# Pooled attention, two gated layers, one core: the second pass gets its own tiles for squares and rows, more raw tiles, and a later load of the plain block's weights

## The chip, the core and the metric

The kernel runs on one NeuronCore of a Trainium2 chip. The metric is the device time of one execution in microseconds. A second execution is recorded by the hardware profiler; all rows shown here are from that one.

## What is computed

Three layers follow each other on 4608 tokens (8 batches of 576), all in float32:

```python
k_p, v_p = mean of k, v over 8 neighbours;  attn = softmax(q @ k_p.T / 8) @ v_p
x   = attn, heads side by side                      # 4608 x 512
h   = (x @ w1) * (x @ w2)                           # 4608 x 1024
y   = (h @ w3) @ w_out                              # 4608 x 512
xn  = y / sqrt(mean(y*y, -1) + 1e-6) * rms_g
out = (silu(xn @ w_gate) * (xn @ w_val)) @ w_out2   # inner width 1536
```

Every matmul is done on pairs of float32r tiles, a rounded part ("hi") and the rest ("lo"), in three products (helper mm3, lines 104 to 106).

## The kernel before

The inputs are taken in 9 blocks of 512 tokens, and the program has four stages.

**First pass.** While w3 @ w_out is multiplied out to one matrix wp, attention for batch 0 runs; then for each block the function ab makes h, feature by feature, between pieces of the attention for the next batch. Eight blocks store h in memory (hdram); the ninth keeps it on the chip (h8).

**Second pass.** Nine turns, in the order of blocks 8, 4, 5, 6, 7, 0, 1, 2, 3 (the list OB); the text calls them turn 0 to turn 8. A turn has eight steps m, each of four groups of three matmuls of y = wp.T @ h: 96 matmuls. For every second step one piece of h (128 x 1024) is loaded by SyncE's queue (h_load, tile hr, 3 buffers), cast by ACT and subtracted by DVE into a pair hb (h_split, line 1315, 4 buffers). The four results of a turn stand in four PSUM banks; turns alternate between two pools of four banks. At the end of a turn y_end squares the four banks (ACT, L670), copies them out (L678 and L680), stores them, and adds up the squares (DVE, L684). During the next turn the list todo is worked off, one entry per step: sq_split makes a hi and lo pair of the sum of squares (L690, L692), four entries do nothing, then rms multiplies by a vector of ones (L698, L699; the result is put in a bank of the pool that the finished turn used), copies the one row to the chip's memory (L701, "the row copy"), and stores it (sdram<-f, L702, "the row store"). GpSimd's queue loads it back (L704), DVE scales it (L705), GpSimd takes the power -0.5, and stores it to rdram (L709). Block 0, of turn 5, needs its row again during turn 7, as xn_load (L1017) and xn_split (L1027 to L1031).

**Weights prepared beside it.** The gate, value and output weights are turned from float64 words to float32, combined and split by the steps of Conv, gv_steps and o2_steps. From the ninth block on these are called by the Ticker named side, one call per step, 82 calls for 97 entries; the results go to memory in stores of 1 MB on GpSimd's queue (wd, od). Raw words are loaded by SyncE's queue into the tiles xq (2 buffers), and for the output weights also into four tiles cut from the pool x0 (oraw). All float32 work tiles named f, 128 x 512, come from one pool of 5: the squares, the hi and lo of their sum, the row, the raw words' work tile, and later the results of the plain block.

**Third stage.** Block 0 goes plainly through the gated layer (gv, o_mm); its weights are pieces wr, 8 loads of 512 KB that pre_ring issues in turn 0 from step 4. Its results are copied out by put(0), called through end0 inside the first product of the last stage. The other eight blocks go in pairs through a scheme of seven products (quad, o_part) whose sums stand in the tiles acc.

A scheduler orders the instructions on each engine; an engine works its own list strictly in order. The excerpts below are from those lists.

Of the kernel before, what the change touches and what calls it, by code (L numbers as in the profile page):

```python
# [9 lines left out]
F32 = mybir.dt.float32  # L10
# [11 lines left out]
def kernel(  # L22
# [637 lines left out]
    def ybank(i):  # L660
        if turn.get(i, 0) % 2:
            return psum()
        return py_p.tile([P, 512], F32, tag="y", name="y")

    def y_end(i):
        ys = yacc.pop(i)
        sq = []
        for kk in range(KD):
            sq.append(ftile())
            nc.scalar.activation(sq[kk], ys[kk], AF.Square)  # L670
            if i == 0:
                if kk == 0:
                    xr[i, 0] = rtile("xr", F32).rearrange("p (k t) -> p k t", k=KD)
                yc = xr[i, 0][:, kk, :]
            else:
                yc = hxtile("hh" if kk % 2 else "hl").bitcast(F32)
            if kk % 2:
                nc.scalar.copy(yc, ys[kk])  # L678
            else:
                nc.vector.tensor_copy(yc, ys[kk])  # L680
            if i:
                nc.sync.dma_start(out=ydram[i, kk], in_=yc)
            if kk:
                nc.vector.tensor_tensor(out=sq[0], in0=sq[0], in1=sq[kk], op=ALU.add)  # L684
# [11 lines left out]
        def rms():  # L696
            ps = ybank(i) if turn[i] < NB - 1 else psum()
            nc.tensor.matmul(ps[:1], ones, sp[0], start=True, stop=False)  # L698
            nc.tensor.matmul(ps[:1], ones, sp[1], start=False, stop=True)  # L699
            row = ftile()  # L700
            nc.scalar.copy(row[:1], ps[:1])  # L701
# [8 lines left out]

        return [sq_split] + [lambda: None] * 4 + [rms]

# [20 lines left out]
    def xq_raw():  # L733
        return r_ps[0].tile([P, 1024], I32, tag="xq", name="xq", bufs=2)

    def gv_steps(G, s, kp):
# [45 lines left out]

        cs, raws = [], (xq_raw if late else raw_halves())
        for z in range(2):
# [17 lines left out]
    for n, (cs, steps) in enumerate(groups):  # L802
# [3 lines left out]
        if n + 1 not in (4, len(groups)):  # L806
            nxt = groups[n + 1][0]
            steps[4] = lambda f=steps[4], nxt=nxt: (nxt[0].s0(), nxt[1].s0(), f())
        gv_prep += steps
# [64 lines left out]
    def o2_steps():  # L874
        jobs, cells = [], [{} for _ in odram]

        x0raw = []

        def o2_raw():
            if not x0raw:  # L880
                for nm in ("xh", "xl"):
                    t = x0_p.tile([P, KD, TB], F32R, tag=nm, name="oraw").bitcast(I32)
                    t = t.rearrange("p k t -> p (k t)")
                    x0raw.extend([t[:, :1024], t[:, 1024:], None])
            r = x0raw.pop(0)
            x0raw.append(r)
            return xq_raw() if r is None else r

        def row(g, j):
# [4 lines left out]
        for g in range(len(odram)):  # L894
            for j in range(4):
                jobs.append(
                    Conv(
                        w_o2[(4 * g + j) * P : (4 * g + j + 1) * P, :],
                        o2_raw,
                        out=lambda g=g, j=j: row(g, j),  # L900
# [143 lines left out]
    def put(i):  # L1044
        ys = yacc.pop(i)
        for t in range(4):
            o = ftile()
            if t % 2:
# [191 lines left out]
    def o_part(k0, g, i0, steps):  # L1240
        if not accs:
            accs.extend(
                x1_p.tile([P, KD, TB], F32R, tag=nm, name="acc").bitcast(F32)
                for nm in ("xh", "xl")
            )
        X = [psum() for _ in range(2)]
# [66 lines left out]
    for i in range(NB - 2, NB):  # L1313
        for n, (m, s) in enumerate((m, s) for m in range(KF1) for s in range(2)):
# [6 lines left out]
            if i == NB - 2 and n == 10:  # L1321
                for g in range(2):
                    for l, lst in enumerate((wph, wpl)):
                        nc.sync.dma_start(out=lst[g].bitcast(F32), in_=wpdram[g][l])
            if (i, n) > (NB - 2, 13):
                side()
# [7 lines left out]
    for w, i in enumerate(OB):  # L1334
        for m in range(KF1):
# [8 lines left out]
            if m and todo:  # L1344
                todo.pop(0)()
            if w == 0 and m == 4:
                wr += [wtile(wB_p, "wr").rearrange("p k t -> p (k t)") for _ in range(4)]
# [65 lines left out]
    o_mm(0, 2 * NCH - 2)  # L1413
    xn.pop(0)

    def end0():
# [75 lines left out]
```

## Time and profile before

| | us |
|---|---|
| three timed executions: median | 1642.26 |
| lowest, highest | 1640.07, 1647.4 |
| profiled execution, own time | 1649.54 |
| its span, first to last instruction | 1647.5 |
| PE busy in the span | 1595.0 (97%) |
| DVE, ACT, GpSimd busy | 1100.4, 727.3, 85.3 |

PE is busy nearly throughout, so the profile is read for the stretches in which it isn't. A row of a window has the two ends, the length, busy time and instructions of PE, PEld, DVE, ACT and POOL, then the granted share of the TensorE clock (1.00 is 2.4 GHz, a stretch at 1.2 GHz counts 0.5), the busy share of the 16 DMA engines and GB/s. A row of a timeline has start, length, engine, line, operation, tiles, and in brackets the idle time of the engine ahead of it and what ended it.

### The profile page before, as it was taken

How to read it: one execution, taken by the hardware profiler on the slowest of the kernel's cores; microseconds unless marked ns; L12 is line 12 of the kernel's file. 1: busy time of each engine (PE TensorE's matmuls, PEld its weight loads, DVE VectorE, ACT ScalarE, POOL GpSimd, SP SyncE). 2: the span in 40 equal slices, each digit the busy share in tenths (PEclk: the TensorE clock that was granted, in tenths of full speed). 3: DMA queues.
4: the chain of work that ended last, by engine and by line, in shares of the span. 5: the costliest groups of instructions: out<-in, count | busy, mean ns of one | idle time of the engine just before them, and what ended most of it. 6: DMA issues, size and time to landing. Idle time of an engine off the chain costs nothing.

```text
span 1647.5 us, 22285 instructions
## 1 busy us (share of the span) xinstructions
PE 1595.0 (97%) x8114; PEld 1308.0 (79%) x8114; DVE 1100.4 (67%) x1938; ACT 727.3 (44%) x1700; POOL 85.3 (5%) x107
## 2 busy tenths in 40 slices
PE   5899999999999999999899999999999999999998
PEld 2447778877777788887688788988898898898897
DVE  4676698779787158668825264696468747676556
ACT  4776545444442136465523244244335343434422
POOL 1001101010000000111100000000000000000000
PEclk9899999999999999999999999999999999999999
DMA  9858545554571179788777666668666866676652
GB/s 245 259 170 216 114 110 155 132 151 112 147 237 70 65 264 343 257 292 284 272 253 245 192 192 188 202 193 286 187 192 199 287 190 195 197 238 188 194 181 94
DMA packets 191775, 328.96 MB, mean 200 GB/s; under 512 B 52265, under 2 KB 91177, under 8 KB 186034
## 3 DMA queue, kind: packets, MB, share of 16 engines
q1 hardware_dynamic: 172530, 276.10, 53.7%
q0 software_dynamic: 19136, 51.45, 10.7%
q8 instruction: 64, 1.05, 0.3%
q14 instruction: 45, 0.37, 0.1%
HBM read 250.89 MB, written 76.58 MB: 199 GB/s over the span
## 4 chain that ended last, share of the span: by engine, by line
PE 65%; DMA 4%; DVE 3%; issue 1%; ACT 1%; POOL 0%; DVEq 0%; POOLq 0%; ACTq 0%; SPq 0%
PE ps L104 16%; PE ps L105 16%; PE ps L106 16%; PE y L105 3%; PE y L106 3%; PE y L104 3%; PE o L105 2%; PE o L106 2%; PE o L104 2%; DMA sdram<-f 2%; DMA ss<-sdram 1%; PE pa L325 1%; PE pa L428 1%; DVE ost L101 1%; DMA out_dram<-f 0%
## 5 line engine op out<-in xcount | busy, mean ns | idle before, releaser
L104 PE MATMUL ps<-xf,wr 128*128 128x512 f32 x576 | 225.9, 395 | 2.9 <-ACT f L1191 2.8
L105 PE MATMUL ps<-xf,wr 128*128 128x512 f32 x576 | 225.2, 391 | 0.0
L106 PE MATMUL ps<-xf,wr 128*128 128x512 f32 x576 | 224.8, 390 | 0.0
L1071 DVE TENSOR_TENSOR f<-y,f 128x512 f32<-128x512 f32 x48 | 33.1, 690 | 168.0 <-PE y L106 157.2
L368 DVE STREAM_TRANSPOSE aT<-s 32x256 f32<-32x256 f32 x324 | 140.8, 435 | 5.2
L1191 ACT COPY f<-ps 128x512 f32<-128x512 f32 x144 | 84.4, 586 | 127.6 <-PE ps L106 126.5
L104 PEld LDWEIGHTS ps<-xf,wr 128*128 128x128 f32 x576 | 108.5, 188 | 30.4 <-DVE f L1071 5.3
L106 PEld LDWEIGHTS ps<-xf,wr 128*128 128x128 f32 x576 | 108.4, 188 | 23.0
L105 PEld LDWEIGHTS ps<-xf,wr 128*128 128x128 f32 x576 | 108.6, 189 | 21.3
L104 PE MATMUL ps<-xh,w1h 128*128 128x512 f32 x288 | 118.8, 413 | 0.0
L340 ACT ACTIVATE s<-pa,mx 128x72 f32<-128x72 f32 (+1 forms) x280 | 85.4, 331 | 73.2 <-DVE mx L337 73.2
L105 PE MATMUL ps<-xl,w1h 128*128 128x512 f32 x288 | 114.4, 397 | 0.0
L104 PE MATMUL ps<-xh,w2h 128*128 128x512 f32 x288 | 112.8, 392 | 1.4 <-ACT w2h L100 1.4
L106 PE MATMUL ps<-xh,w1l 128*128 128x512 f32 x288 | 113.0, 392 | 0.0
L106 PE MATMUL ps<-xh,w2l 128*128 128x512 f32 x288 | 112.4, 390 | 0.0
L105 PE MATMUL ps<-xl,w2h 128*128 128x512 f32 x288 | 112.2, 390 | 0.0
L634 PE MATMUL wps<-wo,hl 128*128 128x512 f32 x128 | 67.9, 658 | 15.8 <-ACT hl L560 8.4
L572 ACT COPY f<-ps 128x512 f32<-128x512 f32 x72 | 42.9, 599 | 81.0 <-PE ps L106 77.2
L1071 DVE TENSOR_TENSOR f<-ps,f 128x512 f32<-128x512 f32 x96 | 65.0, 687 | 19.8 <-PE ps L106 8.9
L1071 DVE TENSOR_TENSOR acc<-ps,acc 128x512 f32<-128x512 f32 x72 | 48.5, 686 | 33.8 <-PE ps L106 19.1
L106 PE MATMUL ps<-o,hf 128*128 128x256 f32 x240 | 67.9, 283 | 0.0
L105 PE MATMUL ps<-o,hf 128*128 128x256 f32 x240 | 67.9, 283 | 0.0
(244 smaller groups left out, 3934.1 us busy)
## 6 DMA issues: line engine op xcount, KB each, us to landing
wr<-wd SPq DMA_DIRECT2D x168, 512.0 KB
o<-od SPq DMA_DIRECT2D x96, 512.0 KB
wd<-wst POOLq DMA_DIRECT2D x24, 1024.0 KB, 7.1
hr<-hd SPq DMA_DIRECT2D x32, 512.0 KB
od<-ost POOLq DMA_DIRECT2D x12, 1024.0 KB, 7.3
wr<-wd SPq DMA_DIRECT2D x48, 256.0 KB
x1raw<-in_moe_w_dram SPq DMA_DIRECT2D x20, 512.0 KB
hd<-hh SPq DMA_DIRECT2D x36, 256.0 KB
```

What stands on the lines that cost most here:

```text
L101: nc.vector.tensor_tensor(out=lo, in0=src, in1=hi.bitcast(F32), op=ALU.subtract)
L104: nc.tensor.matmul(o, lh, rh, start=first, stop=False, skip_group_check=part)
L105: nc.tensor.matmul(o, lh, rl, start=False, stop=False, skip_group_check=part)
L106: nc.tensor.matmul(o, ll, rh, start=False, stop=last, skip_group_check=part)
L325: nc.tensor.matmul(ps[:n, (p % 2) * 2 * SP : (p % 2 + 1) * 2 * SP], qT_t[t // 2][:, t % 2, p, :n], kT[:, p, :], start=True, stop=True,)
L340: nc.scalar.activation(s_t[t][:n, h, :SP], pv[:, j, :], AF.Exp, bias=mx[:, j, :], accum_out=den_t[t][:n, h, :],)
L368: nc.vector.transpose(aT[32 * kb : 32 * kb + 32, :, s0 + 32 * i : s0 + 32 * i + 32], s_t[t][32 * i : 32 * i + 32, :, 32 * kb : 32 * kb + 32],)
L428: nc.tensor.matmul(ps[j * D : (j + 1) * D, :n], st8["vp", b][:, h * D : (h + 1) * D], st8["aT", b][:SP, h, c0 : c0 + n], start=True, stop= ...
L572: nc.scalar.copy(a0[i, m], ps)
L634: nc.tensor.matmul(wps[i], wt[:, i * P : (i + 1) * P], wo[j // 4][:, j % 4, :], start=j == 0, stop=j == KF1 - 1,)
L1071: nc.vector.tensor_tensor(out=out, in0=in0, in1=in1, op=op)
L1191: nc.scalar.copy(t, bank)
```

## The change

Four things change.

- x0b: the two tiles of pool x0, free after the first pass, are cut into eight pieces. The squares take pieces 0 to 3, the row takes piece 4 or 5 by turn, instead of f tiles. The hi and lo of the sum stay f tiles. rms stands one entry earlier in todo (after step 5 instead of step 6).
- late_raw: at the ninth block, once the first four weight tiles of the first pass (pool wB) are free, they become eight more raw tiles. Late gate, value and output weights take them and the two xq in rotation; the oraw tiles go. The loads of the next group but one are issued when the sums of a group are made.
- The tiles wr, of the same pool wB, are now taken and loaded in turn 8, from step 1 (as the program is written), after the last entry of side.
- put(0) copies into the sum tile acc, which is now taken before the last stage, instead of f tiles.

```diff
+    def bpiece(k):
+        if not x0b:
+            for nm in ("xh", "xl"):
+                t = x0_p.tile([P, KD, TB], F32R, tag=nm, name="x0b")
+                x0b.extend(t[:, u] for u in range(KD))
+        return x0b[k]
-            sq.append(ftile())
+            sq.append(bpiece(kk).bitcast(F32))
-            row = ftile()
+            row = bpiece(4 + turn[i] % 2).bitcast(F32)
-        return [sq_split] + [lambda: None] * 4 + [rms]
+        return [sq_split] + [lambda: None] * 3 + [rms]
+    def late_raw():
+        if not more:
+            return xq_raw()
+        r = more.pop(0)
+        more.append(r)
+        return xq_raw() if r is None else r
-            steps[4] = lambda f=steps[4], nxt=nxt: (nxt[0].s0(), nxt[1].s0(), f())
+            def sums_and_loads(f=steps[4], n=n, nxt=nxt):
+                for n2 in (n + 1, n + 2):
+                    if n2 == n + 1 or (more and n2 < len(groups)):
+                        for c in groups[n2][0]:
+                            if not hasattr(c, "raw"):
+                                c.s0()
+                f()
-            o = ftile()
+            o = accs[0][:, t, :]
+            if (i, n) == (NB - 1, 9):
+                wbt = [wtile(wB_p, "raws").bitcast(I32) for _ in range(4)]
+                for u in range(2):
+                    more.append(None)
+                    for t in wbt:
+                        more.append(t.rearrange("p k t -> p (k t)")[:, u * 1024 : (u + 1) * 1024])
-            if w == 0 and m == 4:
+            if w == NB - 1 and m == 1:
+                side.flush()
                 wr += [wtile(wB_p, "wr").rearrange("p k t -> p (k t)") for _ in range(4)]
```

On ACT, at the end of turn 7. L1030 is a part of block 0's xn_split, hb the cast of a piece of h, ost<-ot the casts of prepared output weights, L701 the row copy, L670 the squares at the turn's end. Before:

```order
L1030 ACTIVATE xnh_6726<-xr,g_col 128x512
L100 CAST hb<-hr 128x1024
L1030 ACTIVATE xnh_6726<-xr,g_col 128x512
L701 COPY f<-y 1x512
L100 CAST ost<-ot 128x2x256
L1030 ACTIVATE xnh_6726<-xr,g_col 128x512
L100 CAST ost<-ot 128x2x256 x3
L670 ACTIVATE f<-ps 128x512 x2
```

Now (L1045, L710 and L679 are the same three lines of code):

```order
L1045 ACTIVATE xnh_6675<-xr,g_col 128x512 x2
L100 CAST hb<-hr 128x1024
L100 CAST ost<-ot 128x2x256 x2
L1045 ACTIVATE xnh_6675<-xr,g_col 128x512
L100 CAST ost<-ot 128x2x256 x2
L100 CAST hb<-hr 128x1024
L710 COPY x0b<-y 1x512
L1045 ACTIVATE xnh_6675<-xr,g_col 128x512
L679 ACTIVATE x0b<-ps 128x512 x2
```

The row copy stood after the first two L1030 and ahead of all ost<-ot casts; now it stands behind four ost<-ot casts, three L1030 and the cast of one more piece of h.

On SyncE's queue, turn 6 (hd_97 and hd_98 are the pieces of h of turns 7 and 8, sdram the row store, oraw and xq raw output weights). Before:

```order
L127 DMA oraw<-in_moe_w_out_dram 128x1024
L127 DMA xq<-in_moe_w_out_dram 128x1024
L1301 DMA hr<-hd_97 128x2x512
L1301 DMA hr<-hd_98 128x2x512 x2
L702 DMA sdram<-f 1x512
L682 DMA ydram<-hl 128x512
L682 DMA ydram<-hh 128x512
L1301 DMA hr<-hd_98 128x2x512
```

Now (L1311, L711 and L982 are h_load, the row store and ring_load; wd_0_1027 and wd_0_1033 are the plain block's first weights):

```order
L1311 DMA hr<-hd_97 128x2x512
L982 DMA wr<-wd_0_1027 128x2x512 x2
L1311 DMA hr<-hd_97 128x2x512 x2
L1311 DMA hr<-hd_98 128x2x512
L982 DMA wr<-wd_0_1033 128x2x512
L711 DMA sdram<-x0b 1x512
L1311 DMA hr<-hd_98 128x2x512
L982 DMA wr<-wd_0_1033 128x2x512
```

The raw loads are gone from here, since they stand earlier; three loads of the plain block's weights come between the loads of h ahead of the row store, and one behind it.

On the same queue in turn 7, f<-rdram being the load of block 0's row. Before:

```order
L1301 DMA hr<-hd_98 128x2x512
L1017 DMA f<-rdram 128x512
L702 DMA sdram<-f 1x512
```

Now:

```order
L1311 DMA hr<-hd_98 128x2x512
L1032 DMA f<-rdram 128x512
L982 DMA wr<-wd_1_1028 128x2x512 x2
L1311 DMA hr<-hd_98 128x2x512
L982 DMA wr<-wd_1_1034 128x2x512 x2
L711 DMA sdram<-x0b 1x512
```

One piece of h and four loads of weights now stand behind the load of block 0's row.

## Rows read from the trace of the kernel before

**Rows 1.** Stretches by turn (0, 1, 6, 7, 8), then 20 us of the pairs.

```profile
619.08:640.84 21.76, 21.76 (x97) 18.02 (x96) 20.30 (x30) 13.77 (x18) 2.13 (x4) 1.00 0.89 329
640.84:663.10 22.26, 22.26 (x99) 18.19 (x98) 15.76 (x23) 13.07 (x20) 1.07 (x2) 1.00 0.96 370
...
752.14:780.34 28.20, 24.17 (x99) 19.01 (x98) 22.02 (x35) 17.35 (x28) 4.69 (x7) 0.94 0.78 280
780.34:804.50 24.16, 22.56 (x99) 18.11 (x98) 18.85 (x31) 14.47 (x24) 3.62 (x5) 1.00 0.79 282
804.50:834.93 30.43, 25.85 (x100) 20.23 (x98) 19.35 (x31) 13.18 (x23) 4.33 (x7) 0.89 0.75 284
940.00:960.00 20.00, 17.20 (x70) 13.69 (x69) 7.78 (x12) 7.78 (x14) 0.00 (x0) 0.91 0.58 186
```

**Rows 2.** PE in order of time: matmuls before which it stood.

```profile
755.80 0.50 PE L104 MATMUL y<-hb,wp 128*128 128x512 f32 x1 [1.45 <-ACT f L701]
...
774.81 0.40 PE L698 MATMUL ps<-f,ones 128*1 128x512 f32 x1 [1.72 <-ACT f L690]
...
776.06 0.59 PE L699 MATMUL ps<-f,ones 128*1 128x512 f32 x1 [0.85 <-DVE f L692]
...
784.14 0.50 PE L104 MATMUL ps<-hb,wp 128*128 128x512 f32 x1 [1.60 <-ACT f L701]
...
808.86 0.50 PE L104 MATMUL y<-hb,wp 128*128 128x512 f32 x1 [2.16 <-ACT f L701]
...
816.79 0.79 PE L105 MATMUL y<-hb,wp 128*128 128x512 f32 x1 [2.42 <-DVE hb L101]
...
943.11 0.79 PE L104 MATMUL ps<-xf,wr 128*128 128x512 f32 x1 [2.80 <-ACT f L1191]
```

**Rows 3.** Waits from turn 0 to turn 8: us in total, times, longest.

```profile
ACT f L670 <- DMA sdram<-f: 16.8, 4, 5.5
```

**Rows 4.** ACT in order of time (columns as in rows 2).

```profile
783.52 0.57 ACT L701 COPY f<-ps 1x512 f32<-1x512 f32 x1
...
805.18 1.04 ACT L100 CAST hb<-hr 128x1024 fp32r<-128x1024 f32 x1
...
811.32 1.64 ACT L100 CAST ost<-ot 128x512 fp32r<-128x512 f32 x3
...
941.84 0.58 ACT L1049 COPY f<-y 128x512 f32<-128x512 f32 x1 [6.29 <-DMA out_dram<-f]
```

**Rows 5.** The chain that ended last, turns 5 to 7: start, us, what.

```profile
738.89 2.05 DMA ss<-sdram
...
757.41 7.04 DMA sdram<-f
...
784.12 3.67 DMA sdram<-f
...
788.87 7.28 issue
```

**Rows 6.** DMA between 729 and 835 us: all queues; issues with us to landing.

```profile
...
DMA packets 9965, 30.45 MB, mean 287 GB/s; under 512 B 1078, under 2 KB 1078, under 8 KB 8235
...
od<-ost POOLq DMA_DIRECT2D x12, 1024.0 KB, 7.3
```

**Rows 7.** DVE from turn 5 to 816.65 us: its waits (us in total, times, longest).

```profile
DVE f L684 <- ACT f L670: 8.6, 2, 4.4
DVE ss L705 <- DMA ss<-sdram: 4.3, 3, 1.9
DVE xr L1027 <- DMA f<-rdram: 2.5, 1, 2.5
```

**Rows 8.** The same stretch as one window (columns as in rows 1).

```profile
729.88:816.65 86.77, 76.70 (x320) 60.87 (x318) 69.55 (x110) 53.39 (x89) 14.65 (x22) 0.96 0.80 282
```

**Rows 9.** DVE in turns 7 and 8, in order of time (columns as in rows 2).

```profile
803.82 0.69 DVE L1027 TENSOR_TENSOR xr<-xr,f 128x512 f32<-128x512 f32 x1 [2.46 <-DMA f<-rdram]
...
815.51 1.22 DVE L101 TENSOR_TENSOR hb<-hr,hb 128x1024 fp32r<-128x1024 f32 x1
```

More of the change, by code (lines that the diff above doesn't have):

```diff
@@ L663, in ybank @@
         return py_p.tile([P, 512], F32, tag="y", name="y")
+    x0b = []
+    def bpiece(k):
[4 more added lines that the diff above has]
+        return x0b[k]
     def y_end(i):
@@ L734, in xq_raw @@
         return r_ps[0].tile([P, 1024], I32, tag="xq", name="xq", bufs=2)
+    more = []
+    def late_raw():
[4 more added lines that the diff above has]
+        return xq_raw() if r is None else r
     def gv_steps(G, s, kp):
@@ L781, in store @@
             ready.add((s, c, kp))
-        cs, raws = [], (xq_raw if late else raw_halves())
+        cs, raws = [], (late_raw if late else raw_halves())
         for z in range(2):
@@ L807 @@
             nxt = groups[n + 1][0]
-            steps[4] = lambda f=steps[4], nxt=nxt: (nxt[0].s0(), nxt[1].s0(), f())
+            def sums_and_loads(f=steps[4], n=n, nxt=nxt):
[5 more added lines that the diff above has]
+                f()
+            steps[4] = sums_and_loads
         gv_prep += steps
@@ L875, in o2_steps @@
         jobs, cells = [], [{} for _ in odram]
[L877 to L887, printed above, removed]
         def row(g, j):
@@ L898, in o2_steps @@
                         w_o2[(4 * g + j) * P : (4 * g + j + 1) * P, :],
-                        o2_raw,
+                        late_raw,
                         out=lambda g=g, j=j: row(g, j),
@@ L1240, in o_part @@
     def o_part(k0, g, i0, steps):
[L1241 to L1245, printed above, removed]
         X = [psum() for _ in range(2)]
@@ L1414 @@
     xn.pop(0)
+    accs.extend(
+        x1_p.tile([P, KD, TB], F32R, tag=nm, name="acc").bitcast(F32) for nm in ("xh", "xl")
+    )
     def end0():
```

## The prediction

> **What bounds the kernel now.** I read the page's totals first: PE is busy for 97% of the span, so a change off PE can only give back time in which PE stands or runs at the lower clock. Then I cut the second pass into its nine turns, from the first matmul of one to the first of the next, and looked at each as a window [rows 1]. Turn 0 takes 21.76 us and turn 1, with the two products by ones, 22.26 us, and PE is busy in all of it; turns 2 to 5 last as long. Turn 6 takes 28.20, turn 7 24.16 and turn 8 30.43 us, and the clock column falls to 0.94 and 0.89. So the stage that the change works on is at its limit for six turns and loses 5.94 + 1.90 + 8.17 = 16.0 us in the last three. What PE waits for there is in the list of its gaps [rows 2]: the row copy L701, whose PSUM bank the next turn needs, three times (1.45, 1.60 and 2.16 us); the hi and lo of the sum of squares (1.72 and 0.85); a piece of h (2.42). One gap more, 2.80 us, lies at the start of the pairs, where ACT works off put(0). The gaps of turn 6 sum to 4.02 us, those of turn 8 to 4.58; the rest of their losses (1.92 and 3.59) is time at 1.2 instead of 2.4 GHz, about 1.8 us for each of three falls. Gaps of 1.45 and 1.60 us cost only themselves.
>
> Why ACT is late is in the waits and in its timeline. The squares waited four times, 16.8 us in total and 5.5 at most, for a row store to land [rows 3]: the row lies in an f tile, the fifth f tile is the next one that the squares want, and the 2 KB store took 3.67 to 7.04 us [rows 5]. Behind the squares on ACT stand the casts of h, the hi of the sum, and the casts of output weights. In put(0) it is the same pool: the second copy on ACT waited 6.29 us for an output store to land, and the copy that frees PE's bank is behind it [rows 4].
>
> **The change part by part.** Squares and row in tiles of their own take away the wait on the row store, all 16.8 us of ACT's. DVE stood for 8.6 us behind it from turn 5 on [rows 7]. The squares keep their number and size, so nothing is added on ACT or DVE.
>
> put(0) into the sum tile takes away the 6.29 us wait, with it PE's 2.80 us and the fall of the clock behind it: the window of 20 us has 0.91, that is 1.8 us lost [rows 1]. **4.6 us.** The tile is free, since the matmuls that read it stand ahead on PE.
>
> The eight new raw tiles and the earlier loads move 8 loads of 512 KB into the ninth block and take the 8 loads wr out of turn 0. I cost both at nothing, and the raw loads' earlier place too: PE is busy in all of turns 0 to 5 [rows 1], so neither place has anything on the path. If that cover were gone, 4 MB at the 287 GB/s of turns 5 to 8 [rows 6] would be 15 us.
>
> The loads wr now fall into turns 6 to 8. On SyncE's queue two of them stand ahead of pieces of h of turns 7 and 8, and one right ahead of block 0's row store. The queue waits there until DVE is done with a raw tile. A piece of h is asked for three pieces ahead, 3 x 5.44 = 16.3 us of PE work (21.76 / 4 each), so PE doesn't see this; the row store does. In the trace a row store behind three loads of h took 3.67 us once and 7.04 once [rows 5]. The Trainium skill, DMA: Bandwidth & Descriptors, section Queues, rings and completion order, says that each engine takes a queue's descriptors in ring order; by it the store waits out the 512 KB load ahead, and the forecast below would be some 2 us later (an estimate, 512 KB at 287 GB/s).
>
> rms one step earlier makes the row 12 matmuls (2.7 us) sooner, if ACT copies it at once. In turn 6 it doesn't: the row copy still stands behind four casts ost<-ot.
>
> Now what is late next. **DVE's budget.** From the start of turn 5 to the piece of h that ended PE's last gap, DVE was busy 69.55 of 86.77 us [rows 8]. Without any gap PE wants that piece 3 x 22.26 + 5.44 = 72.2 us after the start of turn 5. The same operations stand on DVE in the new order, so it may wait only 2.7 us in all, and it waited 4.3 us for the row's way through memory and 2.5 us for block 0's row [rows 7] beside the 8.6 that go. DVE thus becomes as long as PE, and turn 8 can't be whole.
>
> **Block 0's row.** In turn 7 the copy at 783.52 [rows 4] led to the row's use at 803.82 [rows 9], 20.3 us later; one leg, the load back with DVE's place behind it, was 7.28 us there and 2.05 in turn 5 [rows 5]. I take the copy at 0.5 us after the start of turn 7 (before: 3.2 us, after the gap on the weights) and 17 us for the way: in use at 17.5 us. In the new order the row copy of turn 7 stands behind all four casts ost<-ot and one piece of h. In the trace the last of these casts ended at 811.32 + 1.64 = 812.96 [rows 4], 9.1 us after the row's use; the piece of h and the copy add 1.04 and 0.57 us [rows 4]. So, at 10.7 us in all, the copy ends 17.5 + 10.7 = 28.2 us after the start of turn 7. PE wants its bank 2.2 us into turn 8 (it stopped at 808.86 - 2.16 = 806.70, turn 8 having begun at 804.50), that is at 24.5 us. A gap of 3.7 us and one fall of the clock, 1.8: **5.5 us stay** of turn 8's 8.17. The piece of h is then ready in time (in the trace 815.51 + 1.22 - 803.82 = 12.9 us after the row's use [rows 9], so at 30.4; wanted at 27.7 + 5.5 = 33.2). The bounds: with the row in use by 13.8 us nothing stays; with the old 20.3 us from a copy at 3.2 us the gap would be 9.7, and with the clock 11.5 us. Turn 6 loses nothing (DVE enters it with the 8.6 us returned), turn 7 between 0 and its 1.90, and I take 0.5.
>
> Sum: 5.94 + 1.90 + 8.17 + 4.6 = 20.6 us to be had, less 5.5 + 0.5: **14.6 us.** Against the profiled execution's 1649.54 that is 1634.9; that execution is 7.3 us above the median of those timed, so against 1642.26 it is **1627.7 us**.
>
> **The rivals.**
> (1) The whole loss goes: 1642.3 - 20.6 = 1621.7. For it: with the short leg the row's way is 20.3 - 5.2 = 15.1 us, which leaves a gap of 1.8 us, little longer than those that cost only themselves. Against it: the budget above, with 2.7 us to spare.
> (2) The new order of ACT makes turn 8 worse: the row is as slow as before (20.3 us from 3.2), the copy is behind the casts, turn 8 loses 11.5 and turn 7 its 1.90. 20.6 - 13.4 = 7.2 us, 1635.1. For it: DVE is no faster, and the row store still waits behind loads. Against: the copy at 3.2 us was itself a result of turn 6's gaps.
> (3) Slower: the transfers become the bound of turns 5 to 8. The stretch moved 30.45 MB at 287 GB/s in 106 us [rows 6]. The new one has 4.2 MB of wr more and about four raw loads (2.1 MB) less, 32.5 MB; at the 280 GB/s of turn 6 [rows 1] 116 us, where it took 105: 11 us more, with three more falls of the clock (5.4) and without the 4.6 of put: 1654. It decides if pieces of h land over 16.3 us after their issue. Against it: turn 1 moved 370 GB/s with no gap on PE [rows 1], a store of 1 MB lands in 7.3 us [rows 6], and wr isn't wanted before turn 8 is over. The Trainium skill, DMA: Bandwidth & Descriptors, section Specifications, gives about 358 GB/s from memory per core; by it 32.5 MB take 91 us against PE's 89, and the time would be some 2 us over the forecast. Turn 1's 370 (both directions counted) speaks against it as a hard limit.
> (4) The change does nothing on the path: then 1642. The waits named above name the very tiles that change, so this is small.
>
> **How the numbers follow.** Forecast 0.55 (its own range 1622 to 1635, from the bounds of block 0's row), (1) 0.18, (2) 0.20, (3) 0.05, (4) 0.02. 0.5%, or 8.2 us, is about what a measurement can tell from no change: faster is under 1634.1. The forecast, (1) and two fifths of (2) give 0.81 for faster; the rest of (2) and (4) 0.14 for the same; (3) 0.05 for slower. The range takes in (1) and (2) with 2 us: 1621.0 to 1637.0.
>
> **What would show it.** Right: turns 1 to 7 as windows of 22.3 to 23 us; no wait of the squares on a row store; no gap of PE on put(0); one gap of 2 to 5 us early in turn 8 on the row copy, and DVE busy nearly throughout turns 5 to 7. Wrong: turn 8 as short as the others (rival 1), a gap of over 7 us there (2), gaps on pieces of h that wait for a DMA (3), or squares still late for another reason (4).

## The result and the profile after

The changed kernel is slower: 1660.39 us median (1656.27 to 1662.56, 4 runs) beside 1642.52 for the kernel before on the same chip (1640.07 to 1647.4, 4 runs), a ratio of 1.0102 with the 95% interval 1.0069 to 1.0135. The forecast was 1627.7 us. The profiled execution of after took 1658.33 us (span 1656.5), that of before 1649.54; the two lie 8.8 us apart where the medians lie 17.9 apart, since the profiled execution of before was slower than every timed run of it. In the rows PE is TensorE, PEld its weight loads, DVE VectorE, ACT ScalarE, POOL GpSimd and SP SyncE; a small q behind the name marks the engine's sequencer or DMA queue.

The second pass of after as windows by turn (turns 4 to 8; us, then busy us of PE, PEld, DVE, ACT and POOL, granted clock, DMA share, GB/s), and 20 us of the pairs:

```profile
709.48:734.86 25.38, 22.57 (x99) 18.10 (x98) 16.61 (x26) 13.88 (x22) 3.64 (x5) 1.00 0.78 273
734.86:757.12 22.26, 22.26 (x99) 18.18 (x98) 17.54 (x29) 15.07 (x27) 4.17 (x6) 1.00 0.73 268
757.12:782.56 25.44, 22.97 (x99) 17.95 (x98) 21.32 (x36) 14.12 (x23) 4.17 (x6) 1.00 0.68 236
782.56:813.29 30.73, 24.72 (x99) 19.59 (x98) 17.51 (x28) 13.00 (x22) 4.43 (x6) 0.89 0.87 319
813.29:848.40 35.11, 24.07 (x100) 19.25 (x99) 19.71 (x30) 14.26 (x24) 3.78 (x6) 0.85 0.83 280
940.00:960.00 20.00, 20.00 (x90) 16.57 (x89) 4.84 (x7) 7.24 (x12) 0.00 (x0) 1.00 0.81 256
```

Turns 0 to 3 are whole. Against a whole turn of 22.26 us, turn 4 loses 3.12, turn 6 3.18, turn 7 8.47 and turn 8 12.85 (its row ends 0.16 us later than that of rows 1, at the end of the last matmul): 27.6 us, where the kernel before lost 16.0 [rows 1]. The last row is the good news: the stretch of put(0) runs at the full clock, where it had 0.91.

What PE waited for in the second pass of after (us in total, times, longest):

```profile
PE y L104 <- ACT x0b L710: 13.1, 2, 11.0
PE ps L104 <- ACT x0b L710: 6.0, 1, 6.0
PE ps L708 <- DVE f L701: 1.8, 1, 1.8
PE ps L707 <- ACT f L699: 1.0, 1, 1.0
```

The row copy, L701 before and L710 now, ends 19.1 us of gaps, where it ended 1.45, 1.60 and 2.16 [rows 2]. The hi and lo of the sum end 2.8 us in turn 4. The 2.04 us of the row copy in turn 6 stand behind a cast of h that waited 2.19 us for its load, the clearest sign of rival 3. Why the rest is late is in what DVE and ACT waited for in the same stretch:

```profile
ACT f L699 <- DVE x0b L693: 37.2, 6, 9.2
...
DVE ss L714 <- DMA ss<-sdram: 18.2, 3, 8.5
DVE ss L714 <- issue: 16.9, 3, 8.1
```

The squares' wait for a row store [rows 3] is gone; no row of after has it. In its place DVE stands 18.2 + 16.9 = 35.1 us, in six waits, at the scaling of the sum of squares, a 128x4 operation that needs the row back from memory; in the kernel before it stood there 13.0 us in the whole pass. ("issue" is time in which the engine waited for nothing that the profile shows; with an unread copy at this place, further below, all six waits are put down to the load back.) And ACT, which waited 16.8 us for stores, now waits 37.2 us for DVE's adds. DVE in turn 4 of after, in order of time (start, us, what, in brackets the idle time before):

```profile
724.67 0.17 DVE L714 TENSOR_SCALAR ss<-ss 128x4 f32<-128x4 f32 x1 [8.07 <-issue]
724.75 1.48 DVE L693 TENSOR_TENSOR x0b<-x0b 128x512 f32<-128x512 f32 x2
726.15 1.22 DVE L101 TENSOR_TENSOR hb<-hr,hb 128x1024 fp32r<-128x1024 f32 x1
```

The program's order has the scaling between the first add of the next squares and the other two. For 8.07 us DVE does nothing; then two adds and a piece of h follow at once. They were ready. GpSimd issued the load back of that row at 718.45, and in turn 4 of the kernel before at 714.68. There DVE came to the scaling only 0.86 us later, since it stood behind squares that waited for the same row store, and it waited 2.24 us (kernel before):

```profile
714.68 0.56 POOL L704 DMA_DIRECT2D ss<-sdram  x1 [9.17 <-DMA sdram<-f]
...
714.85 0.69 DVE L680 COPY hl<-ps 128x512 f32<-128x512 f32 x1 [4.49 <-ACT f L670]
717.78 0.17 DVE L705 TENSOR_SCALAR ss<-ss 128x4 f32<-128x4 f32 x1 [2.24 <-DMA ss<-sdram]
```

How a stand of DVE reaches PE shows in the chain that ends in turn 7 of after, here in turn 6 (start, us, what):

```profile
767.15 4.12 issue
771.27 0.17 DVE ss L714
771.45 0.59 DVE x0b L693
...
773.58 0.24 DVE ost L101
...
776.51 9.26 DMA od<-ost
```

DVE stands 4.12 us at the scaling, the adds and a piece of the output weights come after it, and the store of those weights is issued at 776.51, 19.4 us into the turn, and lands 9.26 us later.

The chain then goes on, in turns 7 and 8, and shows the whole trip of a row:

```profile
790.59 0.52 SPq L982
...
791.20 5.90 DMA sdram<-x0b
...
798.19 5.85 issue
...
805.82 4.17 DMA rdram<-ss
...
810.04 6.96 DMA f<-rdram
...
825.07 0.95 ACT hb L100
826.01 0.48 ACT x0b L710
...
826.54 0.80 PE y L104
```

Block 0's row is copied at 790.15, 7.6 us into turn 7, and used at 817.02, 26.9 us later; behind its use stand casts of output weights and of h on ACT, then the row copy of turn 8, and PE goes on at 826.54 after 11.04 us. In turn 7 one thing more came ahead of the row copy, on ACT (start, us, what, idle before):

```profile
785.87 2.18 ACT L100 CAST ost<-ot 128x512 fp32r<-128x512 f32 x4 [6.88 <-DMA od<-ost]
...
790.15 0.57 ACT L710 COPY x0b<-ps 1x512 f32<-1x512 f32 x1
```

Four casts of output weights waited 6.88 us for the output-weight store of 776.51 to land, and the copy that frees PE's bank stood behind them. The row store after it took 5.90 us with a load wr right ahead of it on the queue (790.59); in the kernel before it took 3.67 us once and 7.04 once [rows 5]. The prediction weighed a rule of the Trainium skill on that (DMA: Bandwidth & Descriptors, Queues, rings and completion order) by which the row would be some 2 us later; 5.90 lies between the two durations without such a load, so no run here shows it.

### The profile page after: what moved, and what is told of

Read it like the earlier page. It is cut to its first block, busy times and chain, and to the rows that moved or that the text cites. A ratio compares the mean times of both kernels' runs of the same rounds, so it can differ in the third digit from the quotient of the medians.

```text
span 1656.5 us, 22262 instructions
## 1 busy us (share of the span) xinstructions
PE 1593.1 (96%) x8114; PEld 1305.1 (79%) x8114; DVE 1099.1 (66%) x1938; ACT 727.0 (44%) x1700; POOL 85.0 (5%) x107
## 3 DMA queue, kind: packets, MB, share of 16 engines
q0 software_dynamic: 19136, 51.45, 10.7%
## 4 chain that ended last, share of the span: by engine, by line
PE 64%; DMA 5%; DVE 3%; issue 2%; ACT 1%; POOL 0%; SPq 0%; ACTq 0%; POOLq 0%; DVEq 0%
PE ps L104 16%; PE ps L106 16%; PE ps L105 16%; PE y L104 3%; PE y L106 3%; PE y L105 3%; PE o L105 2%; PE o L106 2%; PE o L104 2%; DMA sdram<-x0b 2%; DMA hr<-hd 1%; PE pa L325 1%; PE pa L428 1%; DMA ss<-sdram 1%; DMA od<-ost 1%
## 5 line engine op out<-in xcount | busy, mean ns | idle before, releaser
L104 PE MATMUL ps<-xf,wr 128*128 128x512 f32 x576 | 225.3, 394 | 0.3 <-DVE f L1086 0.2
L104 PE MATMUL y<-hb,wp 128*128 128x512 f32 x160 | 63.1, 395 | 13.1 <-ACT x0b L710 13.1
L1086 DVE TENSOR_TENSOR acc<-ps,acc 128x512 f32<-128x512 f32 x72 | 48.5, 686 | 33.8 <-PE ps L106 19.1
L104 PEld LDWEIGHTS ps<-xh,w1h 128*128 128x128 f32 x288 | 54.8, 190 | 16.6 <-issue 4.7
```

The lines of the kernel that those rows point to most:

```text
L104: nc.tensor.matmul(o, lh, rh, start=first, stop=False, skip_group_check=part)
L1086: nc.vector.tensor_tensor(out=out, in0=in0, in1=in1, op=op)
```

## Experiments

Theory A: DVE, which takes its instructions in order, stands for the row's trip through memory, with the adds, the hi and lo of the sum and the pieces of h behind it. Rivals: B, ACT's row copy is late by itself, because the new order puts it behind the casts of output weights; C, the later loads wr and the earlier raw loads fill the queue. Ratios are against runs of the kernel before on the same chip, whose medians lay between 1645.7 and 1647.0 us. "Second pass" is the time from its first matmul to its last in the one profiled execution; it was 216.0 us before and 227.5 after.

**The scaling on GpSimd** (from the changed kernel)

```
-            nc.vector.tensor_scalar(
+            nc.gpsimd.tensor_scalar(
                 out=ss, in0=ss, scalar1=1.0 / DM, scalar2=1e-6, op0=ALU.mult, op1=ALU.add
```

> Edit: in the changed kernel the scaling of the sum of squares (128x4) stands on GpSimd, ahead of its power there, instead of on VectorE; nothing else. Theory A (VectorE stands at that scaling until the row is back from memory, with the adds of the next squares behind it, and so the hi and lo of the sum, the row and block 0's use of it come late): the waits of 4 to 8.6 us on VectorE go, turn 4 is back at 22.3 us, turns 6 to 8 lose at most 8 us together instead of 24: 1626 to 1637 us. Theory B (ScalarE's row copy, which the new order puts behind the casts of output weights, is late by itself: those casts wait for output stores and for raw tiles): only turn 4's 3.1 us come back, turns 7 and 8 still lose over 15 us: 1652 to 1658. Theory C (the loads of plain weights in turns 6 to 8 and the earlier raw loads fill the queue, so that row, load back and pieces of h land late): the waits move to GpSimd and the row's use is as late as now: 1652 to 1660.

1639.80 us (1634.15 to 1648.01, 10 runs), ratio 0.9967 [0.9947, 0.9988]; second pass 208.9 us. One operation of 0.17 us on another engine turns a kernel 1.0% slower than before into one 0.3% faster. (The profiled execution, 1634.15 us, is the fastest of the ten, so 208.9 us flatters it.) B and C expected 1652 us or more; A's numbers were missed by little, 1637 us at most and at most 8 us lost in turns 6 to 8. The order on ACT has changed with the edit, but the copy of block 0's row, at the start of turn 7, still stands behind all four casts ost<-ot, and after them a piece of h more than in the changed kernel; B fell. So did C as the whole cause, since the same loads stand in this kernel, in nearly the same order on the queue. The store that these four casts wait for is issued 6.6 us into turn 6, not 19.4. Turns 7 and 8 of this kernel as windows:

```profile
770.65:792.91 22.26, 22.26 (x100) 18.19 (x99) 11.16 (x17) 7.91 (x14) 3.01 (x5) 1.00 0.85 286
792.91:824.22 31.31, 25.00 (x100) 19.93 (x99) 18.62 (x28) 13.98 (x24) 4.69 (x7) 0.89 0.79 276
```

Turns 0 to 7 are whole. Turn 8 loses 9.05 us, with a single gap of PE:

```profile
801.42 0.80 PE L104 MATMUL y<-hb,wp 128*128 128x512 f32 x1 [6.31 <-ACT x0b L710]
```

That is the gap on block 0's row that the forecast had (3.7 us), at its place, and larger: the row was copied 1.2 us before turn 7 (0.5 us into it in the forecast), its way took 22.4 us (17), and from its use to the end of the next row copy 9.5 us passed (10.7).

**Products by ones one step later** (from the changed kernel)

```
-        return [sq_split] + [lambda: None] * 3 + [rms]
+        return [sq_split] + [lambda: None] * 4 + [rms]
```

> Edit: in the changed kernel the products by ones stand one step later again, where they stood before the change. The program's order then has VectorE's scaling behind the adds of the next squares, no longer between them. Theory A (VectorE at the load back): turn 4 is back at 22.3 us, the hi and lo of the sum end no gap of TensorE, turns 6 to 8 lose at most 12 us together: 1630 to 1642. Theory B (ScalarE's row copy behind the casts): turn 4 back, turns 7 and 8 still lose over 15 us: 1650 to 1658. Theory C (transfers): as B.

1657.43 us (6 runs), ratio 1.0064 [1.0040, 1.0088]; second pass 225.2 us. Turn 4 is whole again, turns 6 to 8 lose as much as in the changed kernel. The scaling now stands behind the adds, and DVE waits there all the same (waits of DVE in the second pass):

```profile
DVE ss L714 <- issue: 20.4, 3, 7.0
...
DVE ss L714 <- DMA ss<-sdram: 10.4, 3, 4.5
```

30.8 us in place of 35.1. So the earlier step costs turn 4 and little else: what costs is the wait, not its place among the adds. A's numbers failed here, and those of B and C came true (turn 4 back, turns 7 and 8 losing 21.1 us, 1650 to 1658 us). A had expected the losses of turns 6 to 8 to halve, and DVE's waits hardly fell; this run alone doesn't tell the three apart.

**put(0) into the sum tile alone** (from the kernel before)

```
-            o = ftile()
+            o = accs[0][:, t, :]
...
```

> Edit: the kernel before with put(0) into the sum tile alone. All theories: the gap of 2.8 us at put(0) and the fall of the clock behind it go, 4.6 us less than before, 1637 to 1639; the second pass stays as before (turns 6 to 8 lose 16 us). If it isn't faster by 3 us or more, the prediction's term for put was wrong too.

(The sum tile is also taken earlier, as in the changed kernel.) 1643.80 us (10 runs), ratio 0.9987 [0.9968, 1.0007]: 2.1 us less, between 5.3 less and 1.2 more. In the profile the gap is gone, and from the first matmul of the pairs to the last one it is 707.0 us, where the profiled execution of before had 711.7. But another kernel with put(0) as before (below) had 707.9 and no gap there: the stall is not in every execution. The term of 4.6 us was read from one that had it; the interval takes in 4.6 as well as nothing.

**Without the eight raw tiles, wr in turn 0** (from the changed kernel)

```
-            if (i, n) == (NB - 1, 9):
-                wbt = [wtile(wB_p, "raws").bitcast(I32) for _ in range(4)]
...
-            if w == NB - 1 and m == 1:
-                side.flush()
+            if w == 0 and m == 4:
```

> Edit: in the changed kernel the eight more raw tiles are left out, and plain block's weights are loaded in turn 0 as before the change; own tiles, the earlier products by ones and put(0) into the sum tile stay. Theory C (the later loads of plain weights and the earlier raw loads): the second pass loses no more than before the change, 1632 to 1642. Theory A (VectorE at the load back): turn 4 still has its 3 us, the last turns still lose over 15 us: 1648 to 1660. Theory B (row copy behind casts): with fewer raw tiles ScalarE's order changes, and what it gives depends on how many casts stand ahead of the row copy in turns 7 and 8: 1640 to 1660.

1657.26 us (6 runs), ratio 1.0072 [1.0046, 1.0097]; second pass 229.9 us, DVE's waits at the scaling 33.6 us. With neither the late loads nor the early ones it is as slow, and C's time failed. Taken alone that is weak evidence: fewer raw tiles cost time by themselves (ACT waited 23.3 us for raw output weights here), and the losses lie elsewhere, 5.4, 8.0, 7.8 and 7.6 us in turns 4, 5, 6 and 8. C as the whole cause was already out by the first run, which kept all these loads.

**Is it that DVE stands, or that the row waits in DVE's queue?** In the next kernel GpSimd scales, and DVE keeps a copy of the loaded row at the old place, which nobody reads. DVE, ACT, PE and SyncE have the order of the changed kernel.

```
-            nc.vector.tensor_scalar(
-                out=ss, in0=ss, scalar1=1.0 / DM, scalar2=1e-6, op0=ALU.mult, op1=ALU.add
+            seen = const.tile([P, 4], F32, tag="seen", name="seen", bufs=2)
+            nc.vector.tensor_copy(seen, ss)
+            sc = const.tile([P, 4], F32, tag="sc", name="sc", bufs=2)
+            nc.gpsimd.tensor_scalar(
+                out=sc, in0=ss, scalar1=1.0 / DM, scalar2=1e-6, op0=ALU.mult, op1=ALU.add
             )
...
```

> Edit: in the changed kernel the scaling of the sum of squares goes to GpSimd, into a tile of its own, and VectorE keeps a copy of the loaded row at the same place of its order, which nobody reads. The order on ScalarE, VectorE, TensorE and SyncE is that of the changed kernel, so VectorE waits for the load back as it does there, but the row's way through memory no longer waits for VectorE. Theory A (what costs is that VectorE stands, with the adds, the hi and lo of the sum and the pieces of h behind it): as slow as the changed kernel, 1.006 to 1.012 of the kernel before, with waits of 4 to 8 us at the copy and gaps of TensorE of some 3 us in turn 4. Theory A2 (what costs is that the row waits in VectorE's queue on its way): as fast as with the scaling on GpSimd, 0.994 to 0.999. Theory B2 (moving the scaling helped only because ScalarE's and VectorE's order changed with it): 1.006 to 1.012 as A, but with VectorE's waits at the copy short.

1661.73 us (4 runs), ratio 1.0101 [1.0080, 1.0122]: as slow as the changed kernel, with nothing but a copy that nobody needs. That the two ratios agree so well is partly chance: in the profiled execution (1661.34 us) the pairs took 7 us more than in the other kernels, for a reason that stays open (last section). What counts is the second pass, 225.3 us, beside 227.5 in the changed kernel and 208.9 without the copy. The waits of DVE and PE in it:

```profile
DVE seen L715 <- DMA ss<-sdram: 33.4, 6, 8.9
PE y L104 <- ACT x0b L710: 9.3, 1, 9.3
...
PE ps L104 <- ACT x0b L710: 6.2, 1, 6.2
...
PE ps L708 <- DVE f L701: 1.8, 1, 1.8
PE ps L707 <- ACT f L699: 1.1, 1, 1.1
```

The gaps of turns 4, 7 and 8 are back; turn 6 has none. The chain that ends in the gap of turn 7 now goes through the copy that nobody reads:

```profile
767.62 0.17 DVE seen L715
...
772.87 9.36 DMA od<-ost
...
782.33 0.63 ACT ost L100
```

The output-weight store is issued 16.2 us into turn 6, and the four casts wait 7.00 us for it. It is DVE's standing that costs, and A2 fell. B2 had the same time with short waits at the copy; they are 33.4 us long. The copy brings the orders of the changed kernel with it, and no run has these orders without the wait; against the orders alone speak this chain and the experiment with the products by ones one step later, which has others on ACT, DVE and SyncE, waits 30.8 us and is slow too.

**The scaling on GpSimd in the kernel before** (the first edit alone, on the kernel before)

> Edit: the kernel before with the scaling of the sum of squares on GpSimd alone; squares and row stay in the f tiles. Theory A: the squares still wait on ScalarE for the row stores (some 17 us in turns 3 to 8), so the last three turns still lose 10 to 16 us: 0.998 to 1.001 of the kernel before. Rival (VectorE's stand at the load back is what costs in the kernel before too, and own tiles are not needed): the last turns lose at most 8 us: 0.994 to 0.997.

1640.96 us (10 runs), ratio 0.9975 [0.9956, 0.9994], between the two. ACT's wait for row stores fell from 16.8 to 7.1 us, but in the profile the last three turns lost 15.6 us, as theory A had it, with a gap of 9.9 us on the row copy in turn 8, and the second pass was 215.6 us long. So the rival's loss of at most 8 us failed; the scaling's place alone doesn't mend the second pass.

**Block 0's row loaded and used later** (from the changed kernel with the scaling on GpSimd)

```
-            if w == turn[0] + 2 and xs:
+            if xs and (w == turn[0] + 3 or (w, m, len(xs)) == (turn[0] + 2, 5, 5)):
```

> Edit: the changed kernel with the scaling on GpSimd, and block 0's row loaded at step 5 of turn 7 and used from turn 8 on, instead of loaded at step 0 of turn 7 and used at steps 1 to 4. Theory A (after the scaling moved, only block 0's row holds ScalarE and VectorE up: VectorE stood 10.2 us and ScalarE 9.7 us for it in turn 7, and the gap of 6.3 us in turn 8 is behind that): the gap in turn 8 falls under 2 us, the second pass is 5 to 9 us shorter than with the scaling alone: 0.990 to 0.994 of the kernel before. Rival (the row copy of turn 8 is late because the casts of output weights ahead of it wait for output stores): the gap stays at 4 us or more: 0.995 to 0.998. Second rival: the use in turn 8 delays the first gate products: a new gap of over 2 us behind turn 8.

1639.24 us (10 runs), ratio 0.9964 [0.9947, 0.9981], no faster than without the edit; theory A's expectation failed, and the first rival's came true (a gap of 4 us or more, 0.995 to 0.998). In the profile (second pass 214.1 us) neither engine stood over 2.6 us for the row, but PE had gaps of 2.99 and 7.86 us on the row copy, because casts ahead of it waited for output-weight stores (ACT, second pass):

```profile
ACT ost L100 <- DMA od<-ost: 23.5, 3, 10.3
```

GpSimd issues those stores, and GpSimd was busy with the row (GpSimd in turns 6 and 7):

```profile
754.79 9.18 POOL L717 TENSOR_TENSOR ss<-ss,mhalf 128x4 f32<-128x4 f32 x1
...
764.87 1.09 POOL L943 DMA_DIRECT2D od<-ost  x2
...
789.43 3.78 POOL L714 TENSOR_SCALAR ss<-ss 128x4 f32<-128x4 f32 x1 [4.71 <-DMA ss<-sdram]
...
795.22 1.09 POOL L943 DMA_DIRECT2D od<-ost  x2
```

The pieces were whole when DVE had finished them, at 759.5 and 790.8, so the stores were issued 5.3 and 4.4 us late, and each landed some 4.6 us after its issue. About half of the two long waits (9.57 and 10.29 us) is thus GpSimd's occupation with the row, the rest the stores' own time. In turn 8 2.56 us of ACT's time more went to block 0's row, whose load took 8.40 us. The power took 9.18 us in the first case and 1.0 to 1.5 in the others; why stays open.

**No raw tiles, scaling on GpSimd**

> Edit: the changed kernel with the scaling on GpSimd, but without the eight more raw tiles and with plain block's weights loaded in turn 0. It tells what those two parts of the change are worth once VectorE no longer stands. Theory A (they have nothing on the path): within 3 us of the kernel with all parts and the scaling on GpSimd, 0.995 to 0.999 of the kernel before. Rival (two raw tiles hold the conversion of output weights up, and with it the casts ahead of the rows): gaps of over 3 us in turns 5 to 8, 1.000 to 1.008.

1642.65 us (10 runs), ratio 0.9972 [0.9956, 0.9988], which looks like "nothing on the path" (theory A's range), though the profile's second pass was 214.2 us, with gaps on the hi of the sum (2.59) and a piece of h (5.69). The last pair of runs below decides it otherwise.

**No trip at all.** To take the trip away, and not only shift who waits, the sums were made token by token: four fp32 matmuls with the summed squares as weights and a column of ones as data give 128x4 in PSUM, and DVE scales that. The hi and lo of the sum, the row copy, the row store and the load back are gone.

```
-            nc.tensor.matmul(ps[:1], ones, sp[0], start=True, stop=False)
-            nc.tensor.matmul(ps[:1], ones, sp[1], start=False, stop=True)
...
+            for c in range(4):
+                nc.tensor.matmul(
+                    ps[:, c : c + 1],
+                    sq[0][:, c * P : (c + 1) * P],
+                    ones_f,
+                    start=c == 0,
+                    stop=c == 3,
+                )
...
-            nc.gpsimd.dma_start(out=rdram[i].rearrange("(p c) -> p c", p=P), in_=ss)
+            nc.gpsimd.dma_start(out=rdram[i].rearrange("(c p) -> p c", p=P), in_=ss)
```

> Edit: in the changed kernel the sum over features is made by four matmuls with the summed squares as weights and a column of ones as moving data, all in fp32, so that it comes out as 128x4, tokens on partitions; VectorE scales it straight from PSUM. The split of the sum into hi and lo, the row copy, the row store and the load back are gone; the power, the store of the result and its load for block 0 stay. Theory A3 (what costs is an engine that stands, in order, for the row's trip through memory: VectorE in the changed kernel; GpSimd, with the output-weight stores behind it, where the scaling was moved there): no engine waits for a trip, output-weight stores are issued on time, the second pass loses at most 5 us: 0.987 to 0.993 of the kernel before. Rival (the casts of output weights wait for stores that are slow by themselves, or block 0's use holds the engines up): gaps of 4 us or more stay in turns 7 or 8: 0.994 to 0.998.

> Edit: the same sums in the kernel before, with put(0) into the sum tile; squares stay in the f tiles, two raw tiles and the two others as before, plain block's weights in turn 0. Without a row store nothing holds an f tile for it. Theory A3: the squares no longer wait although they have no tiles of their own; the second pass loses at most 6 us: 0.988 to 0.994 of the kernel before. Rival (own tiles and more raw tiles are needed for it): squares or conversions wait, 0.995 to 1.000.

Both missed: 1655.46 us (10 runs), 1.0055 [1.0034, 1.0075], and 1658.19 us (6 runs), 1.0069 [1.0044, 1.0094]. In the first, turns 1 to 6 are even, at 22.71 us from start to start; then DVE stands 13.72 us for block 0's row. The store of the result now writes pieces of 4 bytes, and it takes that long to land (DMA issues in the second pass, median us to landing, and DVE):

```profile
rdram<-ss POOLq DMA_DIRECT2D x8, 2.0 KB, 11.4
```

```profile
801.31 0.69 DVE L1044 TENSOR_TENSOR xr<-xr,f 128x512 f32<-128x512 f32 x1 [13.72 <-DMA f<-rdram]
```

The Trainium skill says, under DMA: Bandwidth & Descriptors, Rules for kernel authors, that a last dimension that isn't contiguous becomes one descriptor per element. This store's last dimension isn't contiguous in memory. The trace counts no descriptors; what bears on the rule is the duration: with 16-byte pieces (later kernels) the store landed in 4.6 us. In the second kernel ACT waited 23.3, 10.1 and 9.5 us for raw loads of weights into its few raw tiles, which says that those tiles matter; it has the 4-byte store as well, so it doesn't settle it.

**The same with 16-byte pieces**, every fourth token as weights of one matmul; and with block 0's row used later as above.

```
-                    sq[0][:, c * P : (c + 1) * P],
+                    sq[0].rearrange("q (p c) -> q c p", c=4)[:, c],
```

> Edit: the fp32 sums in the changed kernel again, but with every fourth token as weights of one matmul, so that the 128x4 result lies as the row did and is stored in pieces of 16 bytes, not of 4 (the store of 4-byte pieces took 10 us, and VectorE stood 13.7 us for block 0's row behind it). Theory A3 (an engine that stands for a trip costs): VectorE's wait for block 0's row falls to 2 to 6 us, the gap of 7.2 us in turn 7 goes, the second pass is 10 to 18 us shorter than with 4-byte pieces: 0.989 to 0.996 of the kernel before. Rival (the casts of output weights, which waited 11.5 us for output-weight stores in turn 6, set the end): gaps of over 6 us stay in turns 7 and 8 together: 0.997 to 1.005.

> Edit: as the one before, and block 0's row is loaded at step 5 of turn 7 and used from turn 8 on. Theory A3: neither engine stands for the row, turns 7 and 8 lose at most 4 us together: 0.987 to 0.992 of the kernel before. Rival (the output-weight stores): 0.997 to 1.005, with gaps in turns 7 or 8 behind casts that wait for them.

1643.65 us, 0.9989 [0.9976, 1.0002], and 1642.10 us, 0.9976 [0.9954, 0.9999] (10 runs each); A3's times failed in both. The rival's range has both, but not the gaps that it named: 1.59 us in the first is the longest. In the second, PE has not one gap in the whole pass, and yet the pass takes 210.4 us: a turn is 23.55 us long, where contiguous weights gave 22.71: weights taken with a stride cost more.

**The same with contiguous weights.** The last add of the squares writes the tokens permuted. (In the expectation the turns of 22.49 us are counted short by one matmul; from start to start they are 22.71, against 23.55 and 22.26.)

```
+                a, b, o = sq[0], sq[kk], sq[0]
+                if kk == KD - 1:
+                    a, b = (z.rearrange("q (p c) -> q c p", c=4) for z in (a, b))
+                    o = sq[1].rearrange("q (c p) -> q c p", c=4)
...
-                    sq[0].rearrange("q (p c) -> q c p", c=4)[:, c],
+                    sq[1][:, c * P : (c + 1) * P],
```

> Edit: as the fp32 sums with block 0's row used from turn 8 on, but the last add of the squares writes its result with the tokens permuted, so that the weights of the four matmuls lie contiguous again (with every fourth token as weights a turn took 23.56 us, with contiguous ones 22.49, with the products by ones 22.26). Theory A3 (the gain that the prediction worked out is there as soon as no engine stands for a trip): turns 1 to 8 of 22.5 us, the second pass some 202 us long against 216 before, with 4 us for put(0): 0.988 to 0.992 of the kernel before. Rival (the gain is eaten elsewhere, by the strided reads of the add on VectorE or by another stage): 0.995 to 1.000.

1636.09 us (1629.92 to 1638.56, 6 runs), ratio 0.9928 [0.9907, 0.9950]: 11.9 us less than before by the ratio (10.0 between the medians), the fastest of these kernels, and just outside A3's range (0.988 to 0.992). Turns 6 to 8 as windows, and the store of the result:

```profile
757.70:780.41 22.71, 22.71 (x105) 18.91 (x104) 20.36 (x31) 12.43 (x21) 4.84 (x6) 1.00 0.92 339
780.41:803.13 22.72, 22.72 (x106) 18.91 (x105) 15.58 (x24) 9.74 (x16) 2.13 (x4) 1.00 0.92 320
803.13:826.16 23.03, 23.03 (x106) 18.99 (x105) 10.83 (x17) 8.09 (x14) 3.26 (x4) 1.00 0.89 326
```

```profile
rdram<-ss POOLq DMA_DIRECT2D x8, 2.0 KB, 4.6
```

PE is busy throughout, at the full clock; the second pass is 203.8 us, 12.2 less than before. Most of the 14.6 us that the prediction looked for was there, in a kernel without the trip.

**And without the raw tiles** (the edit of "Without the eight raw tiles, wr in turn 0" on top of that)

> Edit: as the one before, without the eight more raw tiles and with plain block's weights loaded in turn 0 as before the change; squares keep their own tiles. If the raw tiles and the later weights carry part of the gain, conversions wait for raw loads (in the kernel before with fp32 sums ScalarE waited 7.8 to 15 us for them) and TensorE has gaps of 3 us or more in turns 3 to 8: 0.996 to 1.006 of the kernel before. If they carry nothing: 0.988 to 0.993, as the one before.

1640.58 us (10 runs), ratio 0.9965 [0.9947, 0.9983], 4.5 us more between the medians. In the profile the second pass is 212.3 us, 8.5 more, with gaps of 2.71 us at most in turns 7 and 8; that execution (1644.71 us) was one of the slowest of its ten, so 8.5 is too much. ACT stood for the raw loads:

```profile
ACT xq L144 <- DMA xq<-in_moe_w_out_dram: 27.1, 4, 11.1
```

So the raw tiles with the later wr do carry part of the gain, once nothing stands for the row. The intervals of the two ratios overlap a little; the waits are clear.

## Why the prediction was wrong, step by step

**The step that failed** is DVE's budget: "it may wait only 2.7 us in all, and it waited 4.3 us for the row's way through memory". The 4.3 us were read in the old order and carried into the new one. From the start of turn 5 on DVE waited 15.5 us there in after (4.72, 4.12 and 6.66), and 7.1 us for block 0's row where it had waited 2.5. In the kernel before, the landing of the row store released two things at once: the squares on ACT, with DVE's adds behind them [rows 3, rows 7], and the load back on GpSimd. So in turns 3 to 6 DVE came to the scaling 0.9 to 1.4 us after the load back was issued, and in turn 7 5.8 us after. With the squares in tiles of their own nothing holds DVE back: in turns 3 to 7 it came between 2.7 us before that issue and 0.1 us after.

Over the six waits it came 16.8 us earlier in sum, measured from the issue, and stood for that time. The other 5.3 us are the loads back, which took longer (median over all loads back, from issue to landing 5.3 us in the second pass, 3.0 before); why they did, no run shows. From the row copy to the scaling it took 12.4 us in turn 7 of the kernel before (783.52 to 795.94) and 13.7 in turn 7 of after (790.15 to 803.83), on the mean of turns 3 to 7 12.4 and 13.0: the trip hardly changed, only who stood for it. I counted a wait as taken away, 16.8 us on ACT, that moved to DVE, whose waits at the scaling grew from 13.0 to 35.1 us. The copy that nobody reads showed it, since it alone brings the loss of the second pass back.

**"rms one step earlier makes the row 12 matmuls (2.7 us) sooner"**: taken as harmless. The order put the scaling between the adds, and turn 4, which I had as whole, lost 3.1 us. A step later it is whole.

**Block 0's row.** The place and the mechanism were right, and so was the warning of rival 2: the row copy of turn 8 stands behind the casts. The sizes were off: the copy was at 7.6 us into turn 7, not 0.5, the way to its use 26.9 us, not 17, the gap 11.04 us, not 3.7. The copy was late by DVE's stand in turn 6, through the output-weight store; of turn 6 the prediction said that it loses nothing (3.18 us measured), of turn 7 at most 1.90 (8.47). Without DVE's stand the way was still 22.4 us and the gap 6.31, so the 17 us were too short in any case. Rival 2 had 11.5 us lost in turn 8 (12.85 measured), but 1.90 in turn 7 (8.47 measured) and nothing in turns 4 and 6 (6.3 measured), so it too came out faster than before. I had made both with a DVE that waited little.

**put(0)**: the gap went, as said. The term of 4.6 us was 2.1 us when timed alone, with an interval that reaches from 5.3 to below nothing; the one profiled execution that I read had the stall, and another kernel's, with put(0) as before, had not.

**Raw tiles and wr "at nothing"**: nothing to be seen next to DVE's waits (1.0072 without them, 1.0102 with them, and the intervals overlap), but 4.5 us between the medians (8.5 of the second pass, in one execution each) when those are gone. The cover I named, a busy PE in turns 0 to 5, says nothing on turns 7 and 8, where ACT waits for raw loads.

**Rival 3, transfers**: not the bound. Without the trip PE ran without a gap while from turn 5 on 328 GB/s were moved on the mean, more than the 287 of the kernel before [rows 6].

**The chances.** Slower had 0.05, all of it with rival 3. A rival of the kind "a wait that takes the place of the one removed" was worked out for ACT's row copy only, and not for the next engine that needs the same row.

## What to carry to other kernels

When a wait on a transfer is taken away, follow the same data to its next reader: time the whole trip from its first instruction to that reader's, and ask which engine will now stand for it and what is queued behind. A wait measured behind another wait is not its length. An operation that needs a round trip through memory belongs on an engine with nothing urgent behind it (GpSimd had the output-weight stores there), or the trip should not exist; here four small matmuls took its place and brought what the change alone had not.

## What the hardware showed that was not expected

A store of 2 KB in pieces of 4 bytes landed after 11.4 us (median of 8), in pieces of 16 bytes after 4.6. Four fp32 matmuls of one column with strided weights made a turn 23.55 us long, with contiguous ones 22.71, against 22.26 with the two products by ones over 512 columns. And in the profiled execution of the kernel with the unread copy the pairs took 714.5 us where all the others but the kernel before (711.7) took 707 to 708, spread evenly over them, at a granted clock of 1.00 and with 0.1 us of gaps: what slowed it stays open, and it warns against reading a few us from two single executions.
